# Moving GpSimd's loads ahead of the normalisations in a fused attention and feed-forward kernel

## The chip, the cores and the metric

The kernel runs on one core of a Trainium2 chip. The metric is the device time of one execution in microseconds. A core has a matrix engine (PE, with its weight loads shown apart as PEld), a vector engine (DVE), a scalar engine (ACT), GpSimd (POOL) and a sync engine (SP) that here issues transfers only. Each works through its own list of instructions, and they wait for one another by semaphores.

## The reference, cut to what matters

Eight batches of eight heads, 576 positions, 64 values per head. Scores under a threshold near the row's maximum are dropped before the softmax; the attention output of all heads is then the input of a feed-forward layer with a gated activation.

```python
scores = scale * q @ k.T
thresh = max(scores, axis=-1) - tau
scores = where(scores >= thresh, scores, -1e9)
attn = exp(scores - max(scores)); attn /= sum(attn) + 1e-9
x = attn @ v                       # (8, 8, 576, 64) -> (4608, 512)
h = x @ w_in                       # 512 -> 2048
out = (h * clip(h + 3, 0, 6) / 6) @ w_out
```

## The kernel before

The work is cut into 16 "quads" of four heads (two per batch) and each quad into 9 slots of 2 x 128 rows of scores: 144 slots, numbered n. One slot's softmax goes round the engines. PE computes the scores; DVE copies them out of the matrix memory and takes the maximum; GpSimd makes the bias from it; ACT masks by that bias and takes the exponential one slot later; DVE inverts the sum; GpSimd normalises to bf16. Then the probabilities are transposed, either by PE (odd slots up to 19, `on_chip`) or by a DMA.

```python
def sm_max(sl):                      # cut: allocation of tiles
    for i, ps in enumerate(sl.tiles):
        nc.vector.tensor_scalar(out=sl.s[:, i, :]..., in0=ps[:, :, 0:HALF], ..., accum_out=sl.m[:, i:i + 1])
        nc.gpsimd.tensor_scalar(out=sl.bias[:, i:i + 1], in0=sl.m[:, i:i + 1], scalar1=-scale, scalar2=tau, ...)

def sm_mask(sl, i): nc.scalar.activation(out=s, in_=s, func=Act.Prelu, bias=sl.bias[:, i:i + 1], ...)
def sm_exp(sl, i):  nc.scalar.activation(out=s, in_=s, func=Act.Exp, accum_out=sl.rsum[:, i:i + 1])

def sm_norm(sl):
    for i in range(2):
        nc.gpsimd.tensor_scalar(out=pn[:, i, :], in0=sl.s[:, i, :], scalar1=sl.rinv[:, i:i + 1], ...)
    if not sl.on_chip:
        nc.sync.dma_start_transpose(out=sl.dst, in_=pn[:]...)
```

GpSimd also issues those loads that turn float32 in memory into bf16 on the chip. They wait in two lists: `casts` has the 32 loads of the feed-forward weights (16 of `w_in`, 16 of `w_out`, 128 rows by 512 columns each), `vcasts` four loads of v for each batch.

```python
def load_v(b):                       # 2 loads of vm, 2 of vr
    for g in range(2):
        vcasts.append(lambda g=g: nc.gpsimd.dma_start(out=vm[:, g * 4:g * 4 + 4, :], in_=v[b, ...]))
    for a in range(2):
        vcasts.append(lambda a=a: nc.gpsimd.dma_start(out=vr[...], in_=v[b, :, 512:S, :]...))
```

The loop over the slots, in the order in which it writes the engines' lists:

```python
N1 = 22
for n, sl in enumerate(queue):
    # cut: allocations; load_v(0) stands ahead of the loop
    if slot == 0 and g == 1 and b + 1 < B:        # first slot of each odd quad
        load_v(b + 1)
    if prev is not None:
        for i in range(2): sm_exp(prev, i)
    sm_max(sl)                                    # maximum and bias of slot n
    if slot != 8 and todo1:                       # feed-forward, first matmul, two chunks of 128 of the 2048
        h = mm1(item); r = mm1_relu(h, on_act=(slot in (0, 1, 3, 5))); mm1_gate(item, h, r)
        todo2.extend(then)
    copies = pe_transpose(queue[n - 2]) if n > 1 and queue[n - 2].on_chip else None
    if prev is not None: sm_recip(prev)
    if copies: copies()
    # feed-forward, second matmul: part p of a tile of 128 rows reads chunks 4p to 4p+3 of w_out
    # cut: pieces is 1, or 0 in slot 3, and 2 at times in slots 0 and 1
    for _ in range(pieces):
        if todo2:
            mm2_part(bb, mt, part)
            if part == 3: outs += mm2_out(bb, mt, on_act=False)
    for i in range(2): sm_mask(sl, i)
    # cut: transposes of q and k for the next pair, attention times v
    queue[n + 1].tiles = scores(...)              # scores of slot n + 1
    if prev is not None: sm_norm(prev)            # normalisation of slot n - 1
    start(loads, 1)                               # loads by the sync engine
    if n < 4 or n > 12:
        start(vcasts, 1)
    if n > 3:
        start(casts, 1 if n < 24 else 2)
    prev = sl
```

`start(jobs, n)` issues the first n of a list. The feed-forward layer of the first batch begins in slot 23, with its second matmul in slot 31.

Of the kernel before, what the change touches and what calls it, by code (L numbers as in the profile page):

```python
# [21 lines left out]
def kernel(  # L22
# [20 lines left out]
    N1 = 22  # L43
# [31 lines left out]
    casts = []  # L75
    vcasts = []
# [40 lines left out]
    def load_v(b):  # L117
        vm = v_pool.tile([P, H, 4 * D], BF16, tag="vm", name="vm")
        vr = vrs[b % 2]
        vsb[b] = (vm, vr)  # L120
        for g in range(2):
            vcasts.append(lambda g=g: nc.gpsimd.dma_start(
                out=vm[:, g * 4:g * 4 + 4, :],
                in_=v[b, g * 4:g * 4 + 4, 0:512, :].rearrange("h (p t) d -> p h (t d)", t=4)))
        for a in range(2):
            vcasts.append(lambda a=a: nc.gpsimd.dma_start(
                out=vr[a * 64:(a + 1) * 64, a, :, :],
                in_=v[b, :, 512:S, :].rearrange("(hp a) p d -> a p hp d", a=2)[a]))
# [21 lines left out]
    def start(jobs, n):  # L150
        for _ in range(min(n, len(jobs))):
            jobs.pop(0)()
# [72 lines left out]
    def transpose_k(pair):  # L225
        ps = main_pe(nat[pair // 2][1], pair)
        return lambda: copy_out(kT_of(pair)[:, 64:576], ps[:])
# [46 lines left out]
    def sm_max(sl):  # L274
        sl.s = s_pool.tile([P, 2, S], F32, tag="s", name="s")
        sl.m = stat_pool.tile([P, 2], F32, tag="m", name="m")
        sl.bias = stat_pool.tile([P, 2], F32, tag="bias", name="bias")
        sl.rsum = stat_pool.tile([P, 2], F32, tag="rsum", name="rsum")
        sl.rinv = stat_pool.tile([P, 2], F32, tag="rinv", name="rinv")
        for i, ps in enumerate(sl.tiles):  # L280
            nc.vector.tensor_scalar(out=sl.s[:, i, :].rearrange("p (a b) -> p a b", a=2), in0=ps[:, :, 0:HALF],  # L281
                                    scalar1=1.0, scalar2=None, op0=Alu.mult, op1=Alu.max,
                                    accum_out=sl.m[:, i:i + 1])
            nc.gpsimd.tensor_scalar(out=sl.bias[:, i:i + 1], in0=sl.m[:, i:i + 1], scalar1=-scale, scalar2=tau,  # L284
                                    op0=Alu.mult, op1=Alu.add)

    def sm_mask(sl, i):
        s = sl.s[:, i, :]
        nc.scalar.activation(out=s, in_=s, func=Act.Prelu, bias=sl.bias[:, i:i + 1], scale=scale,  # L289
                             alpha=REJECT)  # L290

    def sm_exp(sl, i):
        s = sl.s[:, i, :]
        nc.scalar.activation(out=s, in_=s, func=Act.Exp, accum_out=sl.rsum[:, i:i + 1])  # L294

    def sm_recip(sl):
        nc.vector.reciprocal(out=sl.rinv[:], in_=sl.rsum[:])  # L297
# [15 lines left out]
    def pe_transpose(sl):  # L313
        ps = ps_h.tile([P, 2, 1024], BF16, tag="h", name="pt")
        ps = ps[:].rearrange("p a b -> p (a b)")[:, 0:2 * S].rearrange("p (c t) -> p c t", t=P)
        pn = sl.pn[:].rearrange("p a b -> p (a b)")
        for c in range(9):
            nc.tensor.transpose(ps[:, c, :], pn[:, c * P:(c + 1) * P], identb[:])
        return lambda: nc.vector.tensor_copy(out=sl.dst, in_=ps)
# [32 lines left out]
    def mm1(item, pool=None):  # L352
        b, ni, c0, w = item
        hps = (pool or ps_h).tile([P, 2, 512], F32, tag="s" if pool else "h", name="h")
        for n in range(2):
            for ki in range(KI):
                nc.tensor.matmul(hps[:, n, 0:w], w_in_sb[:, ki, (ni + n) * P:(ni + n + 1) * P],  # L357
                                 xT[b][:, ki, c0:c0 + w], start=(ki == 0), stop=(ki == KI - 1))
        return hps[:, :, 0:w]


    def mm1_relu(hps, on_act):
        w = hps.shape[2]
        r = r_pool.tile([P, 2, 320], F32, tag="r", name="r")[:, :, 0:w]
        if on_act:
            nc.scalar.activation(out=r, in_=hps, func=Act.Relu, bias=three[:])  # L366
        else:
            nc.vector.tensor_scalar(out=r, in0=hps, scalar1=3.0, scalar2=0.0, op0=Alu.add, op1=Alu.max)  # L368
        return r

    def mm1_gate(item, hps, r):
        b, ni, c0, w = item
        c0 += (b % 2) * S
        nc.vector.scalar_tensor_tensor(out=gbuf[:, ni:ni + 2, c0:c0 + w], in0=r, scalar=6.0, in1=hps,  # L374
                                       op0=Alu.min, op1=Alu.mult)
# [3 lines left out]
    def mm2_part(bb, mt, part, pool=None):  # L379
        if part == 0:  # L380
            if pool:
                o_ps[0] = pool.tile([P, 2, 512], F32, tag="s", name="o")[:, 0, :]
            else:
                o_ps[0] = ps_o.tile([P, d_model], F32, tag="o", name="o")[:]
        for ni in range(part * 4, part * 4 + 4):
            nc.tensor.matmul(o_ps[0], gbuf[:, ni, mt * P:(mt + 1) * P], w_out_sb[:, ni, :],  # L386
                             start=(ni == 0), stop=(ni == NI - 1))
# [51 lines left out]
    for n, sl in enumerate(queue):  # L439
        quad, slot = sl.quad, sl.slot  # L440
        b, g = divmod(quad, 2)
        now = n
        if slot in (0, 4):
            pts[2 * quad + slot // 4] = pt_pool.tile([P, 9, 512], BF16, tag="pT", name="pT")
        if slot == 8:
            ptr[quad] = ptr_pool.tile([P, 9, P], BF16, tag="pR", name="pR")
        if quad == 0 and slot == 0:
            load_quad(1)
        if slot == (4 if quad else 8) and quad + 2 < NQUAD:
            load_quad(quad + 2)  # L450
        if slot == 0 and g == 1 and b + 1 < B:
            load_v(b + 1)
        if prev is not None:
            for i in range(2):
                sm_exp(prev, i)
        sm_max(sl)

        if slot != 8 and todo1:
            item, then = todo1.pop(0)
            h = mm1(item)  # L460
            r = mm1_relu(h, on_act=(slot in (0, 1, 3, 5)))
            mm1_gate(item, h, r)
# [3 lines that stand above are left out]
            sm_recip(prev)  # L466
        if copies:
            copies()
        outs = []


        pieces = 0 if slot == 3 else 1
        if slot == 0:
            second = True
        if second and slot < 2 and len(todo2) > 1 and todo2[0][1] == todo2[1][1]:
            pieces, second = 2, False
        for _ in range(pieces):
            if todo2:
                bb, mt, part = todo2.pop(0)
                mm2_part(bb, mt, part)  # L480
                if part == 3:
                    outs += mm2_out(bb, mt, on_act=False)
        for i in range(2):
            sm_mask(sl, i)
        evict = None
        nxt = 2 * quad + 2
        if slot == (1 if quad else 2):
            evict = transpose_q(2 * quad + 1)
        elif slot == (2 if quad else 3):
            evict = transpose_k(2 * quad + 1)  # L490
        elif n == 1:
            evict = transpose_rest(0, of_k=False)
        elif slot == 3 and quad > 0:
            av_main(2 * quad - 1)
        elif slot == 4 and quad > 0:
            av_rest(quad - 1)
            if quad % 2 == 0:
                todo1.extend(moe_of(quad // 2 - 1))
        elif slot in (5, 6, 7) and quad + 1 < NQUAD:
            if slot == 5:  # L500
                alloc_qk(quad + 1)
                evict = transpose_q(nxt)
            elif slot == 6:
                evict = transpose_k(nxt)
            else:
                evict = transpose_rest(quad + 1)
        elif slot == 8:
            av_main(2 * quad)
        if evict:
            evict()  # L510
        if n == 0:
            warm_up(8)
        if n + 1 < len(queue):
            queue[n + 1].tiles = scores(queue[n + 1].quad, queue[n + 1].slot)
        if n < 8:
            warm_up(6)
        if prev is not None:
            sm_norm(prev)
        flush()
        late.extend(outs)  # L520
        start(loads, 1)
        if n < 4 or n > 12:
            start(vcasts, 1)
        if n > 3:
            start(casts, 1 if n < 24 else 2)
        prev = sl

    for i in range(2):
# [78 lines left out]
```

## Time and profile before

| | |
|---|---|
| time, median of 3 | 560.93 us (560.43 to 561.46) |
| span of the profiled execution | 558.7 us |
| busy: PE, PEld | 530.6, 309.2 us |
| busy: ACT, DVE, POOL | 469.7, 424.7, 305.3 us |
| bias on POOL | 288 of 189 ns |
| normalisation on POOL | 288 of 745 ns |
| issue of a load on POOL: `vm`, `vr`, `w_in`, `w_out` | 16 each, of 804, 650, 572, 559 ns |

A line of the table of groups gives source line, engine, operation, output and input tiles, shapes and count; behind the first bar the busy time in us and the mean in ns; behind the second the idle time of the engine just before it, with what ended most of it. A line of the timeline gives start in us, length in us, engine, source line, operation and count, and in brackets how long the engine sat idle before it and what released it. L284 is the bias, L289 the mask, L294 the exponential, L302 the normalisation, L281 the maximum, L318 PE's transposes, L260 the scores, L386 the second matmul of the feed-forward layer, and L122, L126, L143 and L147 the loads of `vm`, `vr`, `w_in` and `w_out`. [...]

### The profile page before, as it was taken

How to read it: one execution, taken by the hardware profiler on the slowest of the kernel's cores; microseconds unless marked ns; L12 is line 12 of the kernel's file. 1: busy time of each engine (PE TensorE's matmuls, PEld its weight loads, DVE VectorE, ACT ScalarE, POOL GpSimd, SP SyncE). 2: the span in 40 equal slices, each digit the busy share in tenths (PEclk: the TensorE clock that was granted, in tenths of full speed). 3: DMA queues.
4: the chain of work that ended last, by engine and by line, in shares of the span. 5: the costliest groups of instructions: out<-in, count | busy, mean ns of one | idle time of the engine just before them, and what ended most of it. 6: DMA issues, size and time to landing. Idle time of an engine off the chain costs nothing.

```text
span 558.7 us, 11624 instructions
## 1 busy us (share of the span) xinstructions
PE 530.6 (95%) x3829; PEld 309.2 (55%) x3870; DVE 424.7 (76%) x1041; ACT 469.7 (84%) x999; POOL 305.3 (55%) x646
## 2 busy tenths in 40 slices
PE   8899798799999999999999999999999999999997
PEld 6655455555555555655555555655555565654663
DVE  3787686787878788887978788887978798883440
ACT  4899899798889999899898999899898999984440
POOL 2788878854556555755556555755556555561000
PEclk9999899999999999999999999999999999999999
DMA  5999979976789869978689889977689865454102
GB/s 121 137 120 173 196 128 190 204 142 126 137 158 152 152 136 157 178 149 146 130 148 152 173 131 160 175 147 147 131 145 166 150 144 114 100 109 94 38 20 76
DMA packets 286348, 77.52 MB, mean 139 GB/s; under 512 B 269264, under 2 KB 281808, under 8 KB 286288
## 3 DMA queue, kind: packets, MB, share of 16 engines
q1 hardware_dynamic: 267680, 67.47, 65.3%
q0 software_dynamic: 17408, 8.92, 13.6%
q8 instruction: 30, 0.49, 0.4%
q10 hardware_dynamic: 1200, 0.39, 0.3%
q14 instruction: 30, 0.25, 0.1%
HBM read 36.70 MB, written 9.44 MB: 83 GB/s over the span
## 4 chain that ended last, share of the span: by engine, by line
PE 55%; DVE 11%; ACT 8%; issue 4%; SPq 3%; DMA 2%; POOL 2%; DVEq 0%; POOLq 0%
PE h L357 17%; PE o L386 16%; PE s L260 15%; DVE s L281 5%; PE av L327 3%; ACT s L289 3%; ACT s L294 3%; DMA nq<-in_q_dram 2%; DVE g L374 2%; DVE r L368 2%; ACT r L366 1%; PE s L266 1%; PE tp L214 1%; SPq L310 1%; POOL pn L302 1%
## 5 line engine op out<-in xcount | busy, mean ns | idle before, releaser
L302 POOL TENSOR_SCALAR pn<-s,rinv 128x576 bf16<-128x576 f32 x288 | 211.6, 745 | 133.1 <-DVE rinv L297 57.3
L289 ACT ACTIVATE s<-s,bias 128x576 f32<-128x576 f32 x288 | 206.9, 766 | 36.3 <-POOL bias L284 35.2
L281 DVE TENSOR_SCALAR_CACHE_REDUCE s<-s 128x576 f32<-128x576 f32 x288 | 205.9, 752 | 40.3 <-PE s L260 29.9
L294 ACT ACTIVATE s<-s 128x576 f32<-128x576 f32 x288 | 192.7, 671 | 0.3
L260 PE MATMUL s<-kT,qT 64*128 64x288 f32 x1024 | 169.7, 430 | 5.1 <-DVE s L281 2.8
L357 PE MATMUL h<-xT,w_in_sb 128*128 128x320 bf16 (+1 forms) x1024 | 144.9, 287 | 5.9 <-DVE g L374 5.0
L386 PE MATMUL o<-w_out_sb,g 128*128 128x512 bf16 x535 | 133.5, 379 | 5.2 <-DVE osb L394 3.0
L357 PEld LDWEIGHTS <-w_in_sb 128*128 128x128 bf16 x1024 | 92.1, 97 | 68.9 <-issue 31.9
L374 DVE SCALAR_TENSOR_TENSOR g<-r,h 128x512 bf16<-128x512 f32 (+1 forms) x128 | 96.4, 755 | 41.7 <-ACT r L366 39.9
L260 PEld LDWEIGHTS s<-kT,qT 64*128 64x128 f32 x1024 | 93.7, 186 | 60.9 <-DVE s L281 24.0
L284 POOL TENSOR_SCALAR bias<-m 128x1 f32<-128x1 f32 x288 | 54.4, 189 | 66.6 <-DVE s L281 45.8
L386 PEld LDWEIGHTS <-g 128*128 128x128 bf16 x576 | 55.6, 98 | 57.4 <-issue 9.0
L366 ACT ACTIVATE r<-h,three 128x640 f32<-128x640 f32 (+1 forms) x74 | 54.4, 736 | 20.6 <-PE h L357 19.9
L294 ACT ACTIVATION_READ_ACCUMULATOR s<-s 128x1 f32 x288 | 54.2, 188 | 0.0
L368 DVE TENSOR_SCALAR r<-h 128x512 f32<-128x512 f32 (+1 forms) x54 | 40.5, 751 | 0.0
L394 DVE TENSOR_SCALAR osb<-o 128x512 f32<-128x512 f32 x31 | 21.0, 676 | 21.4 <-PE o L386 21.4
L327 PE MATMUL av<-pT,vm 128*64 128x512 bf16 x256 | 34.6, 393 | 2.0 <-ACT kT L204 2.0
L327 PEld LDWEIGHTS <-vm 128*64 128x64 bf16 x512 | 18.0, 111 | 25.3 <-issue 18.8
L297 DVE RECIPROCAL rinv<-rsum 128x2 f32<-128x2 f32 x144 | 23.0, 160 | 11.3 <-ACT s L294 10.5
L339 DVE CAST xT<-av 128x512 bf16<-128x512 f32 x32 | 21.8, 681 | 6.6 <-PE av L330 6.3
L281 DVE DVE_READ_ACCUMULATOR s<-s 128x1 f32 x288 | 23.9, 83 | 0.0
L266 PE MATMUL s<-kT,qT 64*64 64x288 f32 x256 | 20.1, 415 | 0.7 <-DVE s L281 0.7
(44 smaller groups left out, 241.4 us busy)
## 6 DMA issues: line engine op xcount, KB each, us to landing
km<-in_k_dram SPq DMA_DIRECT2D x64, 128.0 KB, 3.0
out_dram<-osb SPq DMA_DIRECT2D x31, 256.0 KB, 2.4
nq<-in_q_dram SPq DMA_DIRECT2D x96, 72.0 KB, 2.7
vm<-in_v_dram POOLq DMA_DIRECT2D x16, 256.0 KB, 5.6
w_in_sb<-in_moe_w_in_dram POOLq DMA_DIRECT2D x16, 128.0 KB, 4.3
w_out_sb<-in_moe_w_out_dram POOLq DMA_DIRECT2D x16, 128.0 KB, 4.5
pT<-pn SPq DMA_TRANSPOSE x119, 3.4
nq<-in_q_dram SPq DMA_DIRECT2D x14, 128.0 KB, 4.4
```

What stands on the lines that cost most here:

```text
L260: nc.tensor.matmul(tiles[a][:, hf, 0:HALF], qT_of(pair)[a * 64:(a + 1) * 64, t * P:(t + 1) * P], keys(pair, a, hf), start=True, stop=True)
L281: nc.vector.tensor_scalar(out=sl.s[:, i, :].rearrange("p (a b) -> p a b", a=2), in0=ps[:, :, 0:HALF], scalar1=1.0, scalar2=None, op0=Alu.m ...
L284: nc.gpsimd.tensor_scalar(out=sl.bias[:, i:i + 1], in0=sl.m[:, i:i + 1], scalar1=-scale, scalar2=tau, op0=Alu.mult, op1=Alu.add)
L289: nc.scalar.activation(out=s, in_=s, func=Act.Prelu, bias=sl.bias[:, i:i + 1], scale=scale, alpha=REJECT)
L294: nc.scalar.activation(out=s, in_=s, func=Act.Exp, accum_out=sl.rsum[:, i:i + 1])
L302: nc.gpsimd.tensor_scalar(out=pn[:, i, :], in0=sl.s[:, i, :], scalar1=sl.rinv[:, i:i + 1], scalar2=1.0, op0=Alu.mult, op1=Alu.mult)
L327: nc.tensor.matmul(ps[a * 64:(a + 1) * 64, :], vm[:, 2 * hp + a, c * D:(c + 1) * D], pT[:, 5 * a + c, cols], start=(c == 0), stop=False)
L357: nc.tensor.matmul(hps[:, n, 0:w], w_in_sb[:, ki, (ni + n) * P:(ni + n + 1) * P], xT[b][:, ki, c0:c0 + w], start=(ki == 0), stop=(ki == KI ...
L366: nc.scalar.activation(out=r, in_=hps, func=Act.Relu, bias=three[:])
L368: nc.vector.tensor_scalar(out=r, in0=hps, scalar1=3.0, scalar2=0.0, op0=Alu.add, op1=Alu.max)
L374: nc.vector.scalar_tensor_tensor(out=gbuf[:, ni:ni + 2, c0:c0 + w], in0=r, scalar=6.0, in1=hps, op0=Alu.min, op1=Alu.mult)
L386: nc.tensor.matmul(o_ps[0], gbuf[:, ni, mt * P:(mt + 1) * P], w_out_sb[:, ni, :], start=(ni == 0), stop=(ni == NI - 1))
```

## The change

The two calls of `start` for GpSimd's lists move from the end of a slot, behind the normalisation of slot n - 1, to the place right behind the maximum and bias of slot n. GpSimd's order in a slot was bias, bias, normalisation (two instructions), loads; it becomes bias, bias, loads, normalisation. The purpose is to let the loads fall into the time in which GpSimd waits for the reciprocal, and not ahead of the next bias, for which ACT waits.

The amounts change too. A slot now takes from one list only: from `vcasts` in slots 0 to 3, then in every third slot from 12 on and in any slot from 30 on while there is something in it; else from `casts`, one load up to slot 21 and two after that.

```diff
         sm_max(sl)
+        if n < 4 or (vcasts and n >= 12 and (n % 3 == 0 or n >= 30)):
+            start(vcasts, 1)
+        else:
+            start(casts, 1 if n < N1 else 2)
 
         if slot != 8 and todo1:
@@
         flush()
         late.extend(outs)
         start(loads, 1)
-        if n < 4 or n > 12:
-            start(vcasts, 1)
-        if n > 3:
-            start(casts, 1 if n < 24 else 2)
         prev = sl
```

## Prediction

> **What bounds the kernel now.** I read the page first: its table of costliest groups says what every engine does per slot and what ended its idle time.
>
> ```profile
> L302 POOL TENSOR_SCALAR pn<-s,rinv 128x576 bf16<-128x576 f32 x288 | 211.6, 745 | 133.1 <-DVE rinv L297 57.3
> L289 ACT ACTIVATE s<-s,bias 128x576 f32<-128x576 f32 x288 | 206.9, 766 | 36.3 <-POOL bias L284 35.2
> ```
>
> There are 288/2 = 144 slots. The second line is what the change aims at: ScalarE's mask waits 35.2 us in all for GpSimd's bias. Whether the loads cause that must be read by stage. The busy times by stage split it: from 110 to 505 us PE is busy 386.76 of 395 us and ACT 360.66, with GpSimd only 222.80; before 110 us GpSimd is the fuller one (26.61 of 33 us from 77 to 110). The waits of ScalarE, asked by window, give 2.4 us before 22, 10.3 us (17 times) from 22 to 110, and 22.4 us (51 times) after 110. Of the 64 loads GpSimd issues, 40 lie in slots 4 to 30 (21.8 to 110 us), so the 10.3 us are what this change is about. The timeline of GpSimd shows it best, here slots 27 and 28 (start, length, then the work):
>
> ```profile
> 94.05 0.46 POOL L284 TENSOR_SCALAR bias<-m 128x1 f32<-128x1 f32 x2
> 95.51 1.47 POOL L302 TENSOR_SCALAR pn<-s,rinv 128x576 bf16<-128x576 f32 x2 [1.00 <-DVE rinv L297]
> 96.92 0.80 POOL L122 DMA_DIRECT2D vm<-in_v_dram  x1
> 97.72 1.07 POOL L147 DMA_DIRECT2D w_out_sb<-in_moe_w_out_dram  x2
> 98.86 0.46 POOL L284 TENSOR_SCALAR bias<-m 128x1 f32<-128x1 f32 x2
> ```
>
> Three loads (1.87 us) stand between the normalisation and the next slot's bias, and ScalarE pays for them, in its own timeline:
>
> ```profile
> 99.08 1.44 ACT L289 ACTIVATE s<-s,bias 128x576 f32<-128x576 f32 x2 [1.40 <-POOL bias L284]
> ```
>
> Between bias and normalisation GpSimd had just idled 1.00 us for the reciprocal. A load put there is free.
>
> Taking the start of each slot's bias pair from that timeline, I get the periods: slots 4 to 11 take (45.12 - 21.79)/8 = 2.92 us, 12 to 17 take (65.10 - 45.12)/6 = 3.33, 18 to 22 take 2.96, 23 to 30 take (110.02 - 79.92)/8 = 3.76, and from 31 on about 3.49.
>
> [...] the bias at 98.86 starts only after the load issued ahead of it. So a load costs time in whatever stands behind it, and moving it moves the cost onto the normalisation. [...] the issue is some 0.56 us, the landing comes at 4.5 us. [...]
>
> ```profile
> L147 POOL DMA_DIRECT2D w_out_sb<-in_moe_w_out_dram x16: 536/556/579, 73.0 to 105.9; - x16
> ...
> DMA to landing us min/median/max: 3.3/4.5/7.3
> ```
>
> **The change, part by part.** The instruction lists of PE, DVE, ACT and SyncE stay as they are; only GpSimd's order changes, with the same 64 loads. Counting by the new condition: v of the first batch in slots 0 to 3; one weight load each in 4 to 11, 13, 14, 16, 17, 19, 20 (14 loads); v of batch 1 in 12, 15, 18, 21; two weight loads each in 22 to 26, 28, 29 (loads 15 to 28); v of batch 2 in 27, 30, 31, 32; then the last four weight loads in 33 and 34. Before, the last were out in slot 29.
>
> *(a) Slots 23 to 30: gain.* ScalarE's floor per slot is mask 1.35 plus exponentials 1.32, 2.67 us, plus 0.6 to 0.67 for a relu and about 0.5 for a key copy: summed over 23 to 30 about 25.5 us, against 30.1 measured. GpSimd's sum per slot with two loads is 0.46 + 1.11 + 1.47 + gaps 0.2 = 3.25, so three slots stay there. In this stretch ScalarE waited 4.3 us for bias, and 2.5 us of that (1.40 and 1.14) ahead of the masks at 99.08 and 103.00, behind three loads each. Those two disappear; of the rest about a third. **-3.0 us.**
>
> *(b) Slots 12 to 17: gain.* Slots 13 to 16 had a v load and a weight load each, 0.54 + 0.80 or 0.56 + 0.66, and periods of 3.38, 3.37, 3.26, 3.25. With one load GpSimd needs 2.65. But the loop of (c) then takes over at about 3.0, and slot 17 (3.91) loses its late normalisation. 4 x 0.3 + 0.3: **-1.5 us.**
>
> *(c) Slots with one load, 2 to 11 and 18 to 21: loss.* Up to slot 21 the odd slots are transposed by PE, which waits for the normalisation:
>
> ```profile
> 46.71 0.40 PE L318 MATMUL pt<-identb,pn 128*128 128x128 bf16 x4
> 47.38 0.45 PE L318 MATMUL pt<-identb,pn 128*128 128x128 bf16 x5 [0.28 <-POOL pn L302]
> ```
>
> The second group shows PE standing idle until the second normalisation ends. There is a ring over two slots: scores (PE) to maximum (DVE) to bias to normalisation of the odd slot (GpSimd) to transposes (PE) to the next even scores. From the scores at 42.61 to those at 48.20 it took 5.59 us, 2.8 per slot. In that ring the old load stood after the normalisation, where GpSimd next waited for DVE anyway; the new one stands inside, 0.58 plus 0.08 of gap. Part is slack (DVE started the maximum at 44.05 because of an eviction), so I book 0.3 per even slot, for seven of them (4, 6, 8, 10, 18, 20, 22), and 0.35 for slot 2 before any of that is settled: **+2.5 us.**
>
> *(d) Slot 34: loss, the largest single term.* The first batch's second matmul runs in four parts in slots 31 to 34. Part 3 reads w_out chunks 12 to 15, now issued in 33 and 34. PE's list puts part 3 of slot 34 ahead of the scores of slot 35. Before:
>
> ```profile
> 119.38 1.03 PE L386 MATMUL o<-w_out_sb,g 128*128 128x512 bf16 x4
> ...
> 120.02 0.47 POOL L284 TENSOR_SCALAR bias<-m 128x1 f32<-128x1 f32 x2
> ```
>
> The first line is part 3, the second the bias of slot 34. The last chunk is now issued at 120.02 + 0.47 + 0.07 + 0.56 = 121.1, and lands 3.3 to 4.5 us later, 124.4 to 125.6. Its matmul then ends near 125.5 rather than 120.4. PE, in order, stands still for about 5 us, scores of slot 35 come 5 us later, and the following slots are bound by PE, which cannot catch up. **+5.0 us.**
>
> *(e) v loads of later batches.* 20 loads in odd quads after slot 44. In the first five slots of a quad, with loads, quads 7 and 11 took 17.83 us; quad 15, which has none and no later quad to load, took 17.39. That is at most 0.44 us for each of five batches, not all of it due to the issue. **-1.0 us.**
>
> Sum: -3.0 - 1.5 + 2.5 + 5.0 - 1.0 = +2.0, so 560.9 + 2.0 = **562.9 us**.
>
> **Rivals.** *Loads leave the path everywhere:* all 10.3 us of bias waits before 110 us and some of the 22.4 after go, and the weights come in time: 550 to 554. For it: ScalarE is the fuller engine up to slot 30. Against it: after 110 us no load stands in most slots and the wait is there all the same, and (d) is a plain dependency. *The ring takes over:* the whole 0.66 falls on every even slot from 2 to 20, ten times, +6.6 in place of +2.5, giving 567. For it: PE shows waits for the normalisation in each such pair. Against: the warm-up transposes up to slot 7 leave a little slack. *The stall hides:* weight loads land early in a quieter queue or PE makes up for it: -3, giving 560. Against: in slots 36 to 38 maximum waits for PE's scores.
>
> **Range and chances.** The terms have errors of about 1 (a), 1 (b), 2 (c), 1 (d), 1 (e), together about 3 us; 8 in 10 is 558.5 to 567.5. 2% is 11.2 us, more than three such errors away on both sides: faster 0.02, same 0.95, slower 0.03. By direction alone, slower is the likelier.
>
> **What would show it.** (a) The wait of ScalarE for bias between 77 and 110 us falls from 4.3 to under 2. (b), (c) Slots 13 to 16 at about 3.0 us, slots 4 to 11 at 3.0 to 3.1 rather than 2.92, and longer waits of PE's weight loads for the normalisation. (d) A gap of some 5 us on PE near 120 us before the last matmuls on w_out of the first output tile, with all engines idle. (e) Unchanged periods after slot 45. I am wrong if the gap is under 3 us, if ScalarE sets the early slots after all and (c) vanishes, or if the ring slows them by more than half a microsecond each.

## The result and the profile after

The changed kernel takes 569.25 us (median of 4, 566.22 to 569.65) against 561.19 us before (median of 4): ratio 1.0137, 95% interval 1.011 to 1.0164. It is slower, by 8 us, less than 2% but clear of the scatter. The prediction was 562.9 us with a range up to 567.5.

Two groups from the page of the changed kernel, and the granted PE clock in 40 slices (tenths of full speed) under its busy share:

```profile
L302 POOL TENSOR_SCALAR pn<-s,rinv 128x576 bf16<-128x576 f32 x288 | 211.4, 743 | 109.8 <-issue 63.5
L289 ACT ACTIVATE s<-s,bias 128x576 f32<-128x576 f32 x288 | 207.2, 767 | 34.0 <-POOL bias L284 32.8
...
L386 PE MATMUL o<-w_out_sb,g 128*128 128x512 bf16 x576 | 142.6, 382 | 6.4 <-DMA w_out_sb<-in_moe_w_out_dram 4.0
```

```profile
PE   8898798879999999999999999999999999999997
...
PEclk9999889897999999999999999999999999999999
```

ScalarE waits for the bias 32.8 us instead of 35.2: nearly the same, though the place was changed for its sake. The third line is a wait that was not there before, and the clock line (PEclk) has three 8s and a 7 where the kernel before has a single 8.

From slot 23 to 28, where the loads had been many, the change did what it was to do. Slots 27 and 28 of the changed kernel, on GpSimd and then on ScalarE:

```profile
98.18 0.46 POOL L284 TENSOR_SCALAR bias<-m 128x1 f32<-128x1 f32 x2
98.70 0.80 POOL L122 DMA_DIRECT2D vm<-in_v_dram  x1
99.73 1.46 POOL L302 TENSOR_SCALAR pn<-s,rinv 128x576 bf16<-128x576 f32 x2 [0.23 <-DVE rinv L297]
101.28 0.47 POOL L284 TENSOR_SCALAR bias<-m 128x1 f32<-128x1 f32 x2
```

```profile
101.79 1.43 ACT L289 ACTIVATE s<-s,bias 128x576 f32<-128x576 f32 x2
```

The v load sits inside the wait for the reciprocal, the next bias follows 3.10 us after the last one (4.81 before), and the mask of slot 28 waits for nothing (1.40 us before). These lines show place and amount together: the slot issued three loads before and issues one now. The experiments take the two apart.

What went wrong is seen slot by slot. The start of each slot's bias, from GpSimd's timeline, less the same start in the kernel before, in us:

| at the start of slot | 12 | 15 | 16 | 19 | 20 | 23 | 29 | 32 | 34 | 36 | 45 | 143 |
|---|---|---|---|---|---|---|---|---|---|---|---|---|
| changed kernel | 0.83 | 0.70 | 2.06 | 1.92 | 4.03 | 5.35 | 1.90 | 4.27 | 4.29 | 10.83 | 10.83 | 8.63 |

There are two jumps in slots 15 and 19, a gain from 23 to 28, a jump in slot 31, a large one in 34 and 35, and a slow recovery after 45. PE at the second jump (slot 19):

```profile
69.30 1.43 PE L318 MATMUL pt<-identb,pn 128*128 128x128 bf16 x9 [0.55 <-POOL pn L302]
70.52 1.06 PE L214 MATMUL tp<-identf,nq 128*128 128x128 f32 x4
71.51 2.29 PE L260 MATMUL s<-kT,qT 64*128 64x288 f32 x8
```

The eight score matmuls take 2.29 us. In the kernel before, at a granted clock of 1.00, they took 1.24 us, and the transposes of q 0.61 instead of 1.06:

```profile
67.86 0.61 PE L214 MATMUL tp<-identf,nq 128*128 128x128 f32 x4
68.40 1.24 PE L260 MATMUL s<-kT,qT 64*128 64x288 f32 x8
```

So PE works at about half speed there. And PE in slot 34:

```profile
125.81 0.38 PE L386 MATMUL o<-w_out_sb,g 128*128 128x512 bf16 x1 [1.76 <-DMA w_out_sb<-in_moe_w_out_dram]
126.60 0.38 PE L386 MATMUL o<-w_out_sb,g 128*128 128x512 bf16 x1 [0.42 <-DMA w_out_sb<-in_moe_w_out_dram]
128.77 1.15 PE L386 MATMUL o<-w_out_sb,g 128*128 128x512 bf16 x2 [1.79 <-DMA w_out_sb<-in_moe_w_out_dram]
```

This is part 3 of the first output tile, four matmuls that wait one by one for the chunks issued in slots 33 and 34.

### The profile page after: what moved, and what is told of

Its sections match the earlier page's. It is cut to its first block, busy times and chain, and to the rows that moved or that the text cites. A ratio compares the mean times of both kernels' runs of the same rounds, so it can differ in the third digit from the quotient of the medians.

```text
span 567.3 us, 11665 instructions
## 1 busy us (share of the span) xinstructions
PE 538.8 (95%) x3870; PEld 311.4 (55%) x3870; DVE 426.0 (75%) x1041; ACT 471.0 (83%) x999; POOL 308.4 (54%) x646
## 4 chain that ended last, share of the span: by engine, by line
PE 69%; DVE 7%; ACT 3%; issue 2%; DMA 2%; POOL 2%; DVEq 0%; POOLq 0%
PE h L357 20%; PE o L386 20%; PE s L260 18%; PE av L327 4%; DVE s L281 3%; PE s L266 2%; PE tp L214 2%; DVE g L374 1%; DVE r L368 1%; ACT s L289 1%; POOL pn L302 1%; DMA pR<-pn 1%; ACT r L366 1%; ACT s L294 1%; PE av L330 1%
## 5 line engine op out<-in xcount | busy, mean ns | idle before, releaser
L289 ACT ACTIVATE s<-s,bias 128x576 f32<-128x576 f32 x288 | 207.2, 767 | 34.0 <-POOL bias L284 32.8
L386 PE MATMUL o<-w_out_sb,g 128*128 128x512 bf16 x576 | 142.6, 382 | 6.4 <-DMA w_out_sb<-in_moe_w_out_dram 4.0
L260 PEld LDWEIGHTS s<-kT,qT 64*128 64x128 f32 x1024 | 95.2, 189 | 59.3 <-DVE s L281 22.0
L327 PE MATMUL av<-pT,vm 128*64 128x512 bf16 x256 | 33.7, 385 | 0.8 <-DMA pT<-pn 0.8
L327 PEld LDWEIGHTS <-vm 128*64 128x64 bf16 x512 | 17.5, 110 | 25.8 <-issue 15.5
```

What stands on the lines that cost most here:

```text
L260: nc.tensor.matmul(tiles[a][:, hf, 0:HALF], qT_of(pair)[a * 64:(a + 1) * 64, t * P:(t + 1) * P], keys(pair, a, hf), start=True, stop=True)
L327: nc.tensor.matmul(ps[a * 64:(a + 1) * 64, :], vm[:, 2 * hp + a, c * D:(c + 1) * D], pT[:, 5 * a + c, cols], start=(c == 0), stop=False)
```

## The experiments

In the diffs, "amounts" are how many loads of which list a slot takes, "place" is behind the bias or behind the normalisation. The tables give starts of slots less those of the kernel before, as above. The diffs of "move only" and "weights first" are against the changed kernel, the others against the kernel before, cut; where `gp_loads` comes in, the two old calls of `start` are gone. A profile is one execution; where it was far from its kernel's median, that is said.

### Place and amounts apart, and the weights in time

**Move only:** the old amounts, behind the bias.

```diff
         sm_max(sl)
-        if n < 4 or (vcasts and n >= 12 and (n % 3 == 0 or n >= 30)):
+        if n < 4 or n > 12:
             start(vcasts, 1)
-        else:
-            start(casts, 1 if n < N1 else 2)
+        if n > 3:
+            start(casts, 1 if n < 24 else 2)
```

> The loads stand behind the bias as in the changed kernel, in the amounts of the kernel before, so all weights are out by slot 29 and the stall of slot 34 (d in the prediction) can't be there. Theory A (the move itself costs time up to slot 22, since a load now lies between bias and the normalisation that PE waits for[...]): slots 0 to 22 lose 4 us or more against before, slots 13 to 16 with two loads most; later slots gain some 3; 562 to 565 us. Theory B (the loss up to slot 22 comes from the new amounts, one load per slot, not from the place): slots 0 to 22 as before, 556 to 559 us.

Measured: 571.34 us, ratio 1.0166 (1.0115 to 1.0217), the highest median of all, though its interval overlaps that of the changed kernel.

**Amounts only:** the new amounts, behind the normalisation, with the four last weight loads ahead of the v loads of batch 2 (`n % 3 == 0 and n < 27 or n >= 31` in place of `n % 3 == 0 or n >= 30`).

```diff
         start(loads, 1)
-        if n < 4 or n > 12:
+        if n < 4 or (vcasts and n >= 12 and (n % 3 == 0 and n < 27 or n >= 31)):
             start(vcasts, 1)
-        if n > 3:
-            start(casts, 1 if n < 24 else 2)
+        else:
+            start(casts, 1 if n < N1 else 2)
```

> The new amounts (one load per slot up to slot 21) at the old place behind the normalisation; the four last weight loads are taken ahead of the v loads of batch 2, so that slot 34 has its weights. Theory A (the place costs, the amounts help): slots 0 to 22 are 1 to 2 us shorter than before, 559 to 561 us. Theory B (the amounts cost): slots 0 to 22 lose 4 us, 564 us or more.

Measured: 558.10 us, ratio 0.9948 (0.9935 to 0.9962), faster.

**Weights first:** the changed kernel with that same edit of the condition.

```diff
-        if n < 4 or (vcasts and n >= 12 and (n % 3 == 0 or n >= 30)):
+        if n < 4 or (vcasts and n >= 12 and (n % 3 == 0 and n < 27 or n >= 31)):
```

> The changed kernel with one edit: the last four weight loads go out in slots 29 and 30, ahead of the v loads of batch 2 (31 to 34). Theory A (the second matmul of slot 34 waits for these four): slot 34 falls from 8.95 to about 3.3 us and slot 35 by 0.8, so 569.25 - 6.5 = 562.7 us. Rival: PE's halved clock or the transposes' queue makes the gap by itself; then slot 34 stays over 6 us and the time over 567.

Measured: 561.17 us, ratio 1.0014 (0.9992 to 1.0037).

**Late only:** the old amounts, behind the bias from slot 22 on, behind the normalisation before.

```diff
         sm_max(sl)
+        if n >= N1:
+            # the two old calls of start
...
         start(loads, 1)
+        if n < N1:
+            # the two old calls of start
```

> The amounts of before; the loads stand behind the bias only from slot 22 on, where no slot's probabilities are transposed by PE any more, and behind the normalisation up to slot 21. Theory A (the place costs in slots with PE transposes only): slots 0 to 22 as before, slots 23 to 30 shorter by about 3.4 us, later v loads worth 2.2: 555 to 557.5 us. Rival (the sync engine's queue of transposes takes the gain back, as in slot 31 of the changed kernel, which lost 2.3 us on a late transpose): 559 to 561 us.

Measured: 561.34 us (558.80 to 564.96), ratio 1.0005 (0.998 to 1.0029).

| at the start of slot | 12 | 16 | 20 | 23 | 29 | 30 | 32 | 34 | 36 | 143 |
|---|---|---|---|---|---|---|---|---|---|---|
| move only | 2.80 | 4.18 | 4.98 | 5.77 | 3.84 | 3.91 | 13.63 | 13.56 | 13.80 | 11.60 |
| amounts only | 0.04 | -1.45 | -2.59 | -2.12 | -4.09 | -3.99 | -3.35 | -3.06 | -3.64 | -3.62 |
| weights first | 1.92 | 1.54 | 3.01 | 4.35 | 0.95 | 0.40 | 2.99 | 3.02 | 3.26 | 1.18 |
| late only | 0.27 | 0.30 | -0.94 | -0.87 | -2.75 | -2.66 | 5.77 | 5.79 | 6.03 | 3.96 |

So theory A holds for the first two as far as slot 22: the place costs and the amounts help. The time of amounts only is 0.9 us under the range expected. That of move only is 6 us above it, because slots 30 and 31 lose another 9.7 us (3.91 to 13.63): PE can't multiply by v yet and is busy 2.95 of the 10 us from 110 to 120. The weight loads of that product (PEld L327) waited 9.7 us in all for a DMA transpose, once; the second line has the times from the start of a transpose's issue to its landing:

```profile
  PEld L327: 9.7, 1
...
DMA to landing us min/median/max: 3.2/4.3/14.6
```

Amounts only also tells what the amounts did in slots 23 to 28: they gain 1.97 us there (-2.12 to -4.09) with every load still behind the normalisation, more than half of the 3.45 us that the changed kernel gains.

Weights first shows the stall of slot 34: from the start of 34 to that of 36 it loses 0.24 us, where the changed kernel lost 6.54. Its median fell by 8.1 us, more than the 6.5 expected; its profile also lacks the jump of slot 15 (1.80 to 1.55). Up to slot 26 its instruction lists are those of the changed kernel, yet from the start of slot 4 to that of slot 23 it took 61.24 us and the changed kernel 63.28. The third number from the end is the granted clock, first the changed kernel, then weights first:

```profile
20.00:85.00 65.00, 56.96 (x417) 34.31 (x417) 46.90 (x128) 53.96 (x119) 47.63 (x97) 0.92 0.92 135
```

```profile
20.00:85.00 65.00, 55.52 (x423) 33.17 (x423) 48.27 (x132) 55.93 (x121) 49.65 (x102) 0.97 0.97 142
```

The same instructions took 2.04 us less in the execution with the higher clock.

In late only, the rival came true, and worse than expected: slots 23 to 28 gain 1.9 us and slots 30 and 31 lose 8.4 (its profiled execution took 564.45 us, above the median, so the usual loss is smaller). PE in slot 30:

```profile
108.59 1.92 PE L327 MATMUL av<-pT,vm 128*64 128x512 bf16 x8 [7.60 <-DMA pT<-pn]
```

PE stood 7.60 us for probabilities that a DMA transposes. Up to then the sync engine's queue had been full with hardly a break: those between the lines below add up to 0.29 us (the last line is the landing of its transposes from 60 to 125 us):

```profile
92.89 2.10 SPq L310 DMA_TRANSPOSE pT<-pn  x1
95.03 1.37 SPq L88 DMA_DIRECT2D km<-in_k_dram  x2
96.50 4.02 SPq L310 DMA_TRANSPOSE pT<-pn  x1
100.57 6.71 SPq L92 DMA_DIRECT2D nq<-in_q_dram  x4
107.38 2.74 SPq L310 DMA_TRANSPOSE pR<-pn  x1
...
DMA to landing us min/median/max: 3.2/5.2/12.1
```

The tile that PE waits for is that of slot 25. GpSimd had normalised it by 91.95 us; its transpose was issued at 96.50, behind other transfers, the issue took 4.02 us, and the data came some 8.0 us after that (12.1 us from the start of the issue). So the queue makes up about half of the delay and the transfer itself the other half.

### Is it the DMA traffic of slots 27 to 30

**Late only, v behind the weights:** the v loads of batch 2 in slots 30 to 33.

```diff
         if n >= N1:
-            if n < 4 or n > 12:
+            if not casts:
                 start(vcasts, 1)
```

> Late placement as in the run that moved the loads only from slot 22 on, with one edit: the v loads of batch 2 go out in slots 30 to 33, behind the weights, and not beside them in 27 to 30. In that run slots 23 to 30 gained 2.7 us and slot 30 lost 6.8, waiting for transposed probabilities. Theory A (the transposes stand in the sync engine's queue behind other transfers, and the extra loads at 27 to 30 fill the DMA engines): the wait in slot 30 shrinks to 3 us or less, 557 to 559.5 us. Rival (the pipeline has simply caught up with the transposes; loads have no part in it): slot 30 loses 5 us or more all the same, 560.5 us or more.

Measured: 557.16 us, ratio 0.9937 (0.9918 to 0.9956). Slot 30 loses 2.6 us instead of 6.8, with PE waiting 2.4 us for a transposed tile, and the time is in the range: theory A. (The 2.7 us in the text above are counted from the kernel before; from the start of slot 23 the gain of late only was 1.8.) From slot 30 to 32 a loss of 4.0 us stays (-4.20 to -0.23), where late only lost 8.4: fewer loads in that stretch halve it in these two profiles, of which that of late only was an unusually long execution.

**New amounts, place from slot 31 and from slot 22:** both with the weights ahead of v.

```diff
         sm_max(sl)
+        if n >= 31:             # second version: n >= N1, which is 22
+            gp_loads(n)         # the condition of "amounts only"
...
         start(loads, 1)
+        if not (n >= 31):       # second version: not (n >= N1)
+            gp_loads(n)
```

> The new amounts with the weights ahead of v, at the old place up to slot 30 and behind the bias from slot 31 on (v loads only). Theory A (in slots where GpSimd waits for the reciprocal anyway the place behind the bias is free): 2.2 us less than the same amounts at the old place, 558.1 - 2.2 = 555.9 us, with the quads that have v loads 0.4 us shorter each. Rival (v loads are hidden at either place): 558 us.

Measured: 555.13 us, ratio 0.992 (0.9888 to 0.9951). This and the next have the lowest medians of all versions, below both kernels.

> The new amounts with the weights ahead of v, at the old place up to slot 21 and behind the bias from slot 22 on; the other version of this kind, from slot 31 on, took 555.1 us. Theory A (slots 22 to 30 gain from the place, but what they gain is lost again at slots 30 to 32 in waits for transposed probabilities, since the sync engine's queue sets that pace): slots 23 to 30 are 1 to 3 us shorter, slot 36 is within 1 us of that version, 554.5 to 556 us. Rival (the gain stays): 552 to 553.5 us.

Measured: 555.62 us, ratio 0.9916 (0.9899 to 0.9934).

| at the start of slot | 23 | 27 | 30 | 31 | 32 | 36 | 45 | 81 | 117 | 143 |
|---|---|---|---|---|---|---|---|---|---|---|
| place from 31 | -1.95 | -2.49 | -3.82 | -3.45 | -3.19 | -3.47 | -3.46 | -4.12 | -5.00 | -5.65 |
| place from 22 | -1.95 | -3.12 | -5.91 | -5.07 | -2.75 | -2.49 | -2.48 | -3.14 | -4.02 | -4.67 |

At slot 30 the earlier place is 2.1 us ahead; two slots later it is 0.4 behind. What the slots from 23 to 29 gain is handed back when PE comes to probabilities that are not yet transposed:

```profile
PEld L327 <- DMA pT<-pn: 1.9, 1, 1.9
PEld L327 <- DMA pR<-pn: 1.9, 1, 1.9
```

(waits of place from 22, from 100 to 118 us: sum, times, longest). From slot 45 on the place behind the bias is worth 2.19 us (-3.46 to -5.65; with the same loads behind the normalisation the difference stays between -3.49 and -3.47, in the run "odd slots" below).

### Which normalisation matters

Up to slot 21 in odd slots only, then in even slots only, behind the bias; from 22 on everything behind the normalisation. Amounts as in "amounts only".

```diff
         sm_max(sl)
+        if n < N1 and n % 2 == 1:        # mirror image: n % 2 == 0
+            gp_loads(n)
...
         start(loads, 1)
+        if not (n < N1 and n % 2 == 1):  # mirror image: n % 2 == 0
+            gp_loads(n)
```

> The new amounts with the weights ahead of v; up to slot 21 the loads of odd slots stand behind the bias and those of even slots behind the normalisation, from 22 on all behind the normalisation. Behind an odd slot's bias comes the normalisation of an even slot, which a DMA transposes, not PE. Theory A (only the ring through PE's transposes costs): slots 0 to 22 as with all loads at the old place, 2 to 3 us under before, 558 us. Theory B (any load ahead of a normalisation costs): slots 0 to 22 lose about half of what the changed kernel lost, 561 us or more.

Measured: 557.09 us (557.05 to 557.10), ratio 0.9942 (0.9927 to 0.9957).

> The mirror image: up to slot 21 the loads of even slots stand behind the bias, ahead of the normalisation that PE's transposes wait for, and those of odd slots at the old place. Theory A (the ring): slots 0 to 22 lose 4 us or more against all loads at the old place, with waits of PE for the normalisation and a halved PE clock, 562 to 565 us. Theory B: as the odd slots, 560 to 561 us.

Measured: 563.47 us, ratio 1.0056 (1.0039 to 1.0073).

| at the start of slot | 12 | 15 | 16 | 19 | 20 | 23 | 30 | 36 |
|---|---|---|---|---|---|---|---|---|
| changed kernel | 0.83 | 0.70 | 2.06 | 1.92 | 4.03 | 5.35 | 1.82 | 10.83 |
| odd slots | 0.08 | -0.90 | -1.25 | -2.45 | -2.37 | -1.97 | -4.49 | -3.49 |
| even slots | 0.71 | 0.56 | 1.94 | 1.79 | 3.91 | 5.15 | 3.18 | 3.77 |

Even slots reproduce the changed kernel up to slot 23, jumps and all; odd slots cost next to nothing (-1.97 at slot 23, where amounts only has -2.12). The time of even slots lies in theory A's range, that of odd slots 0.9 us under the 558 us expected. The loss comes from loads ahead of those normalisations that PE's transposes wait for. PE's waits between 40 and 80 us in the two, odd slots first:

```profile
PE pt L318 <- POOL pn L302: 2.0, 7, 0.3
```

```profile
PE pt L318 <- POOL pn L302: 4.7, 11, 0.7
```

### How much of it is PE's clock

Four idle transposes behind the scores of even slots from 8 to 20, in the even-slot run and, as a control, in the odd-slot run.

```diff
         if n < 8:
             warm_up(6)
+        elif n < N1 - 1 and n % 2 == 0:
+            warm_up(4)
```

> The run with loads behind the bias of even slots, with four idle transposes of the identity on PE behind the scores in even slots from 8 to 20, where PE waits for the normalisation. Its losses up to slot 22 came as small steps of under 0.1 us per slot and two jumps of 1.4 and 2.1 us in slots 15 and 19, with matmuls of twice the length. Theory A (the jumps are PE's clock, halved because PE was too little busy): the granted clock stays at 1.00 between 48 and 80 us, both jumps go, and at slot 23 at most 4 us remain against the same fill with loads in odd slots; 559.5 to 561 us. Rival (the jumps are the ring itself, the low clock comes with them and costs nothing): the jumps stay, 563 us or more.

Measured: 561.39 us, ratio 1.0015 (1.0008 to 1.0023); 2.1 us below the run without the fill and 0.4 above the range expected.

> Control: the same four idle transposes in the run with loads behind the bias of odd slots, where PE's clock was at 1.00 throughout these slots. If they cost nothing by themselves, 557.1 us; if they lengthen the ring, 558 to 561 us.

Measured: 558.62 us, ratio 0.9961 (0.995 to 0.9973); the fill costs 1.5 us there.

Busy time by stage (us of the stage, then busy us and instructions of PE, PEld, DVE, ACT and POOL, the granted clock, the DMA share and GB/s), first even slots, then even slots with the fill:

```profile
56.00:60.00 4.00, 3.44 (x15) 1.89 (x14) 2.36 (x5) 2.24 (x6) 2.13 (x4) 0.66 0.98 182
...
68.00:72.00 4.00, 3.34 (x19) 2.17 (x18) 2.88 (x7) 3.61 (x8) 3.70 (x8) 0.62 0.79 133
72.00:76.00 4.00, 4.00 (x17) 2.61 (x15) 2.29 (x7) 2.04 (x6) 1.27 (x4) 0.53 0.70 106
```

```profile
56.00:60.00 4.00, 3.44 (x30) 1.74 (x28) 3.54 (x10) 3.76 (x8) 3.12 (x7) 1.00 1.08 186
...
68.00:72.00 4.00, 3.40 (x27) 2.21 (x26) 3.16 (x8) 3.36 (x9) 3.09 (x7) 1.00 0.60 88
72.00:76.00 4.00, 3.76 (x31) 2.16 (x29) 3.23 (x10) 3.67 (x8) 3.34 (x7) 1.00 0.87 137
```

The clock is the third number from the end. PE is busy the same 3.44 us in the first stage, but does 15 matmuls at 0.66 and 30 at 1.00. With the fill both jumps are gone: from 15 to 16 even slots lost 1.38 us and now gain 0.24, from 19 to 20 they lost 2.12 and now 0.40. At the start of slot 23 the two placements differ by 5.15 + 1.97 = 7.12 us without the fill, and by 2.14 + 1.00 = 3.14 with it. By this yardstick the ring is 3.1 us and the clock 4.0; the medians give 2.8 and 3.6 (563.47 - 557.09 without the fill, 561.39 - 558.62 with it). The split leans on the fill costing both placements alike. If it cost the even slots nothing, the clock would still be 5.15 - 2.14 = 3.0 us. So ring and clock are some 3 to 4 us each. Theory A holds, though the run's profile (of an execution of 564.60 us, above the median) loses another 3.3 us in slots 31 to 34 that this comparison doesn't concern and that was not followed up.

What goes ahead of a fall of the clock can be read from the granted clock. In the changed kernel it falls to 0.50 four times, for 3.41 or 6.83 us (at 55.39, 69.04, 99.76 and 127.07 us), and the starts of these falls are 13.65, 30.72 and 27.31 us apart, 4, 9 and 8 times 3.41. Here are the changed kernel's stretches around its two jumps:

```profile
51.98:55.39 3.41, 2.35 (x13) 1.24 (x14) 3.07 (x11) 3.08 (x8) 2.44 (x6) 1.00 1.31 173
55.39:58.80 3.41, 3.41 (x17) 2.31 (x17) 1.54 (x3) 2.77 (x6) 2.63 (x5) 0.50 1.15 215
65.63:69.04 3.41, 2.18 (x12) 0.97 (x8) 2.17 (x6) 2.42 (x6) 1.79 (x5) 1.00 1.07 154
69.04:75.87 6.83, 6.46 (x28) 4.37 (x30) 4.37 (x13) 4.48 (x12) 3.89 (x10) 0.50 0.63 106
```

PE was busy 69% and 64% of the 3.41 us ahead of the two falls, 66% and 33% ahead of the other two (2.24 and 1.14 us), and in the kernel before 57% ahead of the fall at 59.35 us (1.93 us). The reverse doesn't hold: in move only PE was busy 57% from 63.90 to 67.31 us, and the clock stayed at 1.00.

```profile
63.90:67.31 3.41, 1.94 (x22) 0.99 (x19) 2.28 (x6) 2.46 (x6) 3.10 (x7) 1.00 1.03 172
67.31:70.72 3.41, 2.48 (x16) 1.40 (x15) 2.21 (x6) 2.42 (x7) 1.72 (x5) 1.00 0.95 121
```

With the fill PE was busy 35.78 of the 40 us from 44 to 84 us, in odd slots 35.55, and in even slots without the fill 33.76; the clock stayed at 1.00 in the first two. So these five falls came after stretches with PE busy 69% or less, but not every such stretch brought a fall, and what decides there stays open.

## Why the prediction was wrong

By its own steps, with the differences of the changed kernel's profile, which add up to its 8.63 us:

| step | predicted | measured | from |
|---|---|---|---|
| (b) amounts up to slot 22 | -1.5 | -2.0 | odd slots at the start of 23 |
| (c) ring of PE's transposes, up to slot 22 | +2.5 | +7.1 | even less odd slots: ring and clock 3 to 4 each |
| (a) slots 23 to 28 | -3.0 | -3.45 | 5.35 to 1.90; some 2.0 of it by the amounts |
| given back in slots 29 to 33 | none | +2.4 | 1.90 to 4.29 |
| (d) slots 34 and 35 | +5.0 | +6.5 | 4.29 to 10.83 |
| (e) later v loads | -1.0 | -2.2 | 10.83 to 8.63 |

(The changed kernel reaches 5.35 us at slot 23, and the two parts give -2.0 + 7.1 = 5.1.)

**The step that failed is (c), "so I book 0.3 per even slot, for seven of them".** The ring was the right mechanism and not far off in size: without a change of clock it cost some 3 to 4 us. That it came so near is partly luck, since slots 4 to 11 lost 0.63 us in the changed kernel, where four times 0.3 were booked, and the ring went on costing in slots 12 to 17 (with the fill, even and odd slots are 0.91 us apart at slot 12 and 2.39 at slot 18). But the sum treated PE's waits as waits only. PE waited 4.7 instead of 2.0 us for normalisations between 40 and 80 us (even and odd slots), its busy time fell (33.8 instead of 35.6 of the 40 us from 44 to 84), and in slots 15 and 19 its clock was halved for 3.41 and 6.83 us; with PE kept busy by idle transposes, those two jumps went. The kernel's own warm-up transposes in slots 0 to 7, and the clock of 0.66 between 60 and 64 us in the stages of the kernel before, were the hint; I used the warm-ups only as slack.

That clock also lies in slots 16 and 17 of the kernel before (half from 59.35 to 62.76 us). I put the 3.91 us of slot 17 down to a late normalisation; amounts only gains 1.2 of its 2.1 us in just these two slots, and its clock leaves no room for a fall of 3.41 us there (a mean of 0.996 over 555.1 us is 2.2 us lost, 1.7 of them from 90 to 100 us at 0.83), so (b) may be in part a matter of clock too; this was not taken apart.

No long gap went ahead of these two falls. They show in the lengths (scores in 2.29 instead of 1.24 us) and in the granted clock (0.50 for 3.41 and for 6.83 us), and PE was busy 69% and 64% of the 3.41 us ahead of them; of its waits from 40 to 80 us the longest for a normalisation was 0.7 us and the longest of all 0.9 us. A low share of busy time went ahead of them, not one long gap.

**Missing altogether was the return of gain (a).** The bias waits in that stretch fell as predicted, from 3.8 us (79 to 110 us, before) to 0.8 us (85 to 112 us, after). But the slots behind it need probabilities that DMAs transpose from the sync engine's queue. In the changed kernel PE waited 1.4 us for the rest tile and 0.8 us for a main one, from 108 to 116 us, and the place from 22 shows the same against the place from 31: 2.1 us ahead at slot 30, 0.4 behind at slot 32. What a faster GpSimd would run into was not asked. Nor is the gain itself all due to the place: some 2.0 us of it come with the amounts alone, and the place adds 1.4 (place from 22, -1.95 to -5.36 at slot 29, against 1.97 for place from 31).

**(d) was right in mechanism and short in size.** The gap I forecast at 120 us came at 124, since slot 34 starts 4.29 us later: PE waited 4.0 us for w_out in three waits, and then did the rest at half clock (0.50 from 128 to 132 us), scores in 2.20 instead of 1.20 us. The weights-first run removed it. **(b) and (e) had the right sign**, each under-sized. The sign that I had named for (e), unchanged periods after slot 45, contradicts the gain booked, and it did not come. For (e) I had compared with quad 15, whose surroundings differ; the direct comparison (place from 31) gives 2.2 us for five batches, 0.44 each on average, which was the upper end I named.

As to the signs I had listed: slots 4 to 11 took (45.95 - 21.99)/8 = 3.00 us, as foreseen; slots 13 to 16 (63.10 - 49.27)/4 = 3.46 and not 3.0, mostly by the jump of slot 15, where the clock was halved. The changed kernel's executions fit this too: three took 569.12 to 569.65 us at mean granted clocks of 0.982 to 0.988, the fourth 566.22 us at 0.994. Of the rivals, the ring that takes over (567 us) was nearest, by luck: it booked 6.6 us to the ring alone, which took some 3 to 4.

## What to carry to other kernels

A load issued by a computing engine goes where that engine waits for something else anyway, and not ahead of an instruction that the busiest chain waits for; the same place was nearly free in odd slots and cost 7 us in even ones. When a load is moved or rationed, follow its last copy to its first reader: four late weight chunks cost 6.5 us, more than slots 23 to 28 and the later v loads gained together (3.45 and 2.2). And when a wait on PE grows, count the clock too: look at the granted clock beside PE's busy share before booking a wait at its own length.

## What the runs showed that I had not expected

PE's clock fell to half without any long idle gap: in the changed kernel after 3.41 us with PE busy 2.35 us, where its longest wait from 40 to 80 us was 0.9 us. Four idle transposes per two slots kept it at 1.00 from 44 to 84 us, for 1.5 us of their own. Whether it falls differs between executions with the same instructions: from 20 to 85 us it was 0.92 in the mean in the changed kernel and 0.97 in weights first, and slot 11, with the same lists up to its end, took 3.00 us in the changed kernel and 4.62 in move only. An issue of transfers on the sync engine's queue is not of constant length: from 60 to 125 us a DMA transpose of a main tile took from 1.26 (before) to 5.53 us (move only), with its landing up to 14.6 us, and four loads of q took 2.24 (before, at 117.69 us) and 6.71 us (late only, at 100.57 us), the longer one in a stretch with the higher DMA share (1.55 from 100 to 110 us, against 1.03 from 110 to 120 us before). PE came to wait for these transposes in slots 30 and 31 in every run with the loads of slots 23 to 30 behind the bias, from 0.8 and 1.4 us in the changed kernel to 9.7 us of its weight loads in move only. How these times depend on the traffic was not measured by themselves.
